# Turning keys, queries and attention outputs by DMA transposes in the second half of a windowed-attention and gMLP kernel

## The chip, the cores and the metric

The kernel runs on one core of a Trainium2 chip. The metric is the device time of one execution in microseconds; a profile of one execution gives a span and the work of each engine: PE (TensorE), DVE (VectorE), ACT (ScalarE), POOL (GpSimd) and SP (SyncE, which here only issues DMAs).

## The reference

Attention over 4 batches of 8 heads, 768 tokens and 64 columns a head, with a window of 128 tokens and 4 tokens at the start ("sinks") that every query sees. The result x, 768 x 512 for each batch, goes through a gated feed-forward block.

```python
scores = scale * np.matmul(q, k.transpose(0, 1, 3, 2))
keep = is_sink | in_window            # rel >= 0 and rel < 128, or token < 4
a = softmax(where(keep, scores, -1e9))
x = np.matmul(a, v)                   # heads side by side: 768 x 512
h = gelu_tanh(x @ w_in)               # 768 x 1024
u, v = h[:, :512], h[:, 512:]
v_n = (v - mean) / sqrt(var + 1e-6) * g_ln
gated = u * (w_sg @ v_n + b_sg[:, None])
out = x + gated @ w_out
```

## The kernel before, in words

Two heads make a pair, so there are 16 pairs n = 0 to 15, four to a batch ("block"). HP is 4, NP is 16, NT is 6 (row tiles of 128 tokens). A pair's work is this:

- load: one DMA each for k, q and v, 384 KB in f32. With the order "(p t)" a partition gets six tokens that follow each other, 1,536 bytes in one run; with "(t p)", used for v alone, a partition gets one token of every row tile, six runs of 256 bytes a head. The pool has three buffers for each of k, q and v.
- cast: to bf16, on POOL (G in the code) for all but the first pairs.
- columns: TensorE turns k, and then q, in six 128x128 transposes into a PSUM bank; ACT (A) or DVE (V) copies the bank into kT or qT, [128 columns of two heads, 768 tokens], putting the tokens back in order. kT and qT have two buffers each.
- score: three groups (0, 1, 2) of matmuls into PSUM, each followed by ACT's exp into ex.
- keep_band: what lies outside the window is set to zero, group 0 by a multiplication with a mask on DVE, groups 1 and 2 by selects on POOL.
- values: two halves (c = 0, 1) of matmuls of ex with v; DVE divides by the sum and writes x (x_sb).
- turn_x: TensorE turns the x of the pair in six transposes, DVE copies the bank into xT.

The feed-forward of a block follows when its four pairs are done: open_v and hidden (x times w_in, gelu on ACT, mean and variance on DVE, the normalised vn), and then units called fillers: spatial (w_sg times vn, then gv and gT on DVE) and project (gT times w_out, an output DMA). Fillers of block b are placed, by fill(), between the attention steps of the pairs of block b + 1. The order on every engine is the order in which the code issues; no scheduler moves anything.

The main loop runs over n = 4 to 15 (L653). In iteration n, PE scores pair n, computes values of pair n - 1, turns k and q of pair n + 1 (L670, L678) and x of pair n - 1 (L688), and POOL casts k, q and v of pair n + 2 (L681). At n = 8 and n = 12 ("block") hidden() of the block just ended runs inside the iteration, with values, columns and turn_x of the running pair called between its units (L693). Loads of pair n + 3 are issued at the head of the iteration (L657). All loads, and all outputs but one, are issued by SP, in this order; an instruction of SP that waits holds back what follows.

PSUM tiles of the tag m (transposes, values, feed-forward) share four banks; scores have two tiles of their own. Outputs go through o_sb, six buffers.

Of the kernel before, what the change touches and what calls it, by code (L numbers as in the profile page):

```python
# [9 lines left out]
BF16 = mybir.dt.bfloat16  # L10
# [8 lines left out]
def kernel(  # L19
# [14 lines left out]
    nc = tc.nc  # L34
    V, G, A = nc.vector, nc.gpsimd, nc.scalar

    B, H, S, Dh = q.shape
# [5 lines left out]
    NT = S // 128  # L43
    HP = H // 2
    KD = DM // 128
    KU = DF // 128
    NP = B * HP
# [8 lines left out]
    work = ctx.enter_context(tc.tile_pool(name="work", bufs=2))  # L56
# [28 lines left out]

        nc.sync.dma_start(out=gates[:, i, :], in_=behind)

    def load(n, which, eng=None):
        b, hp = divmod(n, HP)
        src = dict(k=k, q=q, v=v)[which]  # L90
        dst = loads.tile([128, 2, NT, 64], F32, name=which + "_sb")
        order = "h (t p) d -> p h t d" if which == "v" else "h (p t) d -> p h t d"
        (eng or nc.sync).dma_start(
            out=dst, in_=src[b, 2 * hp:2 * hp + 2].rearrange(order, t=NT))
        raw[n, which] = dst

    flat = {}

    def cast(n, which, eng):
        src = raw.pop((n, which))  # L100
        if which == "v":
            eng.tensor_copy(v_bufs[n % NV][:, :, :, 0:64], src)  # L102
            return
        dst = work.tile([128, NT, 128], BF16, name=which + "_bf")
        eng.tensor_copy(dst.rearrange("p t (h d) -> p h t d", h=2), src)  # L105
        flat[n, which] = dst
# [27 lines left out]
    for i in range(WARM):  # L134
# [3 lines left out]
        out=halves[:, :, 0, :], in_=halves[:, :, 0, :], compare_op=ALU.is_ge, fill=DARK,  # L138
        base=0, pattern=[[0, 2], [1, 128]], channel_multiplier=-1)
    G.affine_select(  # L140
        out=halves[:, :, 1, :], in_=halves[:, :, 1, :], compare_op=ALU.is_ge, fill=DARK,
# [44 lines left out]
    def turn_weights(si, eng):  # L186
        ps = bank([128, NT, 128], BF16, "wps")
        for ti in range(NT):
            nc.tensor.transpose(ps[:, ti, :], wsg_sb[ti // HT][:, ti % HT, 128 * si:128 * (si + 1)],
                                iden)  # L190
        if eng is A:
            A.copy(wsgT[:, si, :], ps.rearrange("p t c -> p (t c)"))
        else:
            eng.tensor_copy(wsgT[:, si, :], ps.rearrange("p t c -> p (t c)"))


    def bank(shape, dtype, name):
        return ps_m.tile(shape, dtype, name=name, tag="m")

    kTs, qTs, exps, avs = {}, {}, {}, {}  # L200
    x_sb, xT = {}, {}

    def columns(n, which, eng):
        src = flat.pop((n, which))
        ps = bank([128, NT, 128], BF16, which + "ps")
        for t in range(NT):
            nc.tensor.transpose(ps[:, t, :], src[:, t, :], iden)  # L207
        dst = work.tile([128, S], BF16, name=which + "T")
        o, i = dst.rearrange("c (p t) -> c p t", t=NT), ps.rearrange("c t p -> c p t")
        if eng is A:  # L210
            A.copy(o, i)  # L211
        else:
            eng.tensor_copy(o, i)  # L213
        (kTs if which == "k" else qTs)[n] = dst

    def darkened(n, g):
        return n < HP or (n == HP and g == 0)

# [39 lines left out]
    def keep_band(n, g, eng):  # L258
        if darkened(n, g):
            return  # L260
        ex = exps[n][:, g, :].rearrange("p (l c) -> p l c", l=2)
        w = 512 if g < HT - 1 else 384
        if eng is V:
            m = mask0 if g == 0 else mask
            V.tensor_mul(ex[:, :, 0:w], ex[:, :, 0:w],
                         m[:, 0:w].unsqueeze(1).to_broadcast([128, 2, w]))
            return
        half = ex[:, :, 0:512].rearrange("p l (j s c) -> p l j s c", j=2, s=2)
        diag, prev = half[:, :, :, 0, :], half[:, :, :, 1, :]
        if g == HT - 1:  # L270
            prev = prev[:, :, 0:1, :]
        nj = prev.shape[2]
        eng.affine_select(out=diag, in_=diag, compare_op=ALU.is_ge, fill=0.0, base=0,  # L273
                          pattern=[[0, 2], [0, 2], [1, 128]], channel_multiplier=-1)
        eng.affine_select(out=prev, in_=prev, compare_op=ALU.is_ge, fill=0.0, base=-1,
                          pattern=[[0, 2], [0, nj], [-1, 128]], channel_multiplier=1)

    def begin_x(b):
        x_sb[b] = work.tile([128, HP, NT, 128], BF16, name="x", bufs=3)
        xT[b] = work.tile([128, HP, S], BF16, name="xT")  # L280

    def values(n, c):
        b, hp = divmod(n, HP)
        if hp == 0 and c == 0:
            begin_x(b)
        ex, v_sb = exps[n], v_bufs[n % NV]
        av = bank([128, HT, 2, 65], F32, "av")

        def probs(j, l, half):
            at = 512 * l + 256 * (j % 2) + 128 * half  # L290
            return ex[:, j // 2, at:at + 128]

        first = True
        for m in range(HT):
            i = HT * c + m
            for l in range(2):
                for j, half in ((i, 0), (i - 1, 1)):
                    if j >= 0:
                        nc.tensor.matmul(av[:, m, l, :], probs(j, l, half), v_sb[:, l, j, :],  # L299
                                         start=first, stop=False)  # L300
                        first = False
        for l in range(2):
            sinks = ex[:, HT - 1, 512 * l + 384:512 * (l + 1)]
            to, of = (av[:, 2, l, :], 0) if c == 0 else (av[:, :, l, :], slice(1, 4))
            nc.tensor.matmul(to, sinks, vsink[:, of, n, l, :], start=False, stop=l == 1)  # L305
        rcp = rcps[:, n, c].rearrange("p (i l o) -> p i l o", l=2, o=1)
        V.reciprocal(rcp, av[:, :, :, 64:65])
        V.tensor_mul(  # L308
            x_sb[b][:, hp, HT * c:HT * (c + 1), :].rearrange("p i (l d) -> p i l d", l=2),
            av[:, :, :, 0:64], rcp.to_broadcast([128, HT, 2, 64]))  # L310

    def turn_x(n, eng):
        b, hp = divmod(n, HP)
        ps = bank([128, NT, 128], BF16, "xps")
        for t in range(NT):
            nc.tensor.transpose(ps[:, t, :], x_sb[b][:, hp, t, :], iden)  # L316
        if eng is A:
            A.copy(xT[b][:, hp, :], ps.rearrange("p t c -> p (t c)"))
        else:
            eng.tensor_copy(xT[b][:, hp, :], ps.rearrange("p t c -> p (t c)"))  # L320


    uTs, vns, gTs, v_alls, mvs, rstds = {}, {}, {}, {}, {}, {}
# [207 lines left out]
    def fill(count=1):  # L531
        for _ in range(count):
            if fillers:
                fillers.pop(0)()
# [114 lines left out]

    QUOTA = {4: 3, 5: 3, 6: 3, 7: 2, 8: 1, 9: 3, 10: 3, 11: 3, 12: 3, 13: 3, 14: 3, 15: 3}  # L650
    LAST = NT + 2 * KU - 1
    valued = HP - 1
    for n in range(HP, NP):  # L653
        todo = valued < n - 1
        block = n % HP == 0 and n > HP
        if HP + 3 < n + 3 < NP:
            for which in "kqv":  # L657
                load(n + 3, which)
        if n not in exps:
            score(n, 0, 1)  # L660
        if n == HP:
            for si in range(3, NT):
                turn_weights(si, V)
        keep_band(n, 0, V)
        keep_band(n, 1, G)
        if todo:
            values(n - 1, 0)
        fill(1 if todo else 2)
        if n + 1 < NP and not block:
            columns(n + 1, "k", A)  # L670
        score(n, 2)
        keep_band(n, 2, G)
        if todo:
            values(n - 1, 1)
        if QUOTA[n] > 2 and todo:
            fill()
        if n + 1 < NP and not block:
            columns(n + 1, "q", A if todo else V)  # L678
        if n + 2 < NP:
            for which in "kqv":  # L680
                cast(n + 2, which, G)  # L681
        if QUOTA[n] > 1:
            fill()
        if block:
            open_v(n // HP - 1, 0)
            open_v(n // HP - 1, 1)
        if todo:
            turn_x(n - 1, V)  # L688
        if block:
            open_v(n // HP - 1, 2)  # L690
        valued = n - 1
        if block:
            hidden(n // HP - 1, {1: [lambda: values(n, 0)], 3: [lambda: values(n, 1)],  # L693
                                 5: [lambda: columns(n + 1, "k", A)],
                                 7: [lambda: columns(n + 1, "q", A)], 9: [lambda: turn_x(n, V)],
                                 LAST: [lambda: score(n + 1, 0, 1), lambda: fill(2)]})
            valued = n
    fill()
# [8 lines left out]
    hidden(B - 1, {2: [lambda: seen.update(c=count_good())],  # L707
                   LAST: [lambda: fill(3)]})
    seen["t"] = total(seen["c"])
# [41 lines left out]
```

## Time and profile before

| | |
|---|---|
| time, median of 3 runs | 174.23 us (173.96 to 179.46) |
| the profiled execution | 173.74 us, span 171.9 us, granted PE clock 0.998 |
| PE / DVE / ACT / POOL busy | 161.0 / 134.3 / 114.1 / 75.1 us |
| DMA queue of SP and ACT (q1) | 25.11 MB, 51.7% of 16 engines' span |
| k and q turns (L207), PE | 96 + 96 matmuls |
| x turns (L316), PE | 96 matmuls |

Busy time counts instructions at work, so an engine that is busy may still be waiting for nothing that matters; what sets the end is in the chain of waits. A row of a stage table gives the stretch in microseconds, then its length, then the busy time of each engine with the number of instructions, the granted clock, the busy share of the DMA engines and the rate that they moved. Lines such as L391 are lines of the kernel.

### The profile page before, as it was taken

The page shows a single profiled execution, that of the slowest core. Times are in us where ns is not written, and L with a number is a line of the kernel's source. Part 1 is how long each engine was busy: PE and PEld are TensorE (multiplying, and loading weights), DVE is VectorE, ACT ScalarE, POOL GpSimd, SP SyncE. Part 2 cuts the span into 40 slices and gives each one's busy share as a digit, 9 for nine tenths or more (in the row PEclk, how much of TensorE's full clock was granted, in tenths as well). Part 3 has the DMA queues.
Part 4 walks back from the last instruction along what each step waited for, and adds up shares of the span by engine and source line. Part 5 has one row for each costly group of instructions (what it writes and reads, how often), then busy time and mean ns, then how long its engine had stood idle before and what let it go on. Part 6 is the DMA issues. An engine that isn't in the chain of part 4 may idle for free.

```text
span 171.9 us, 4205 instructions
## 1 busy us (share of the span) xinstructions
PE 161.0 (94%) x1638; PEld 96.8 (56%) x1638; DVE 134.3 (78%) x321; ACT 114.1 (66%) x155; POOL 75.1 (44%) x112
## 2 busy tenths in 40 slices
PE   3989999999899999999999999999999999999970
PEld 3544584565566666565667655564576645555530
DVE  6675575989999986699889993989989969888630
ACT  2189856889687689597886865789787428631130
POOL 6448461124898969600279987000494400000000
PEclk9999999999999999999999999999999999999999
DMA  4999989999999999700199959000300040040243
GB/s 143 328 323 251 182 112 281 202 275 284 308 235 313 277 276 353 178 0 4 67 320 300 259 148 345 35 0 4 122 4 0 28 159 2 0 183 2 99 170 118
DMA packets 40355, 28.75 MB, mean 167 GB/s; under 512 B 26468, under 2 KB 37240, under 8 KB 40328
## 3 DMA queue, kind: packets, MB, share of 16 engines
q1 hardware_dynamic: 36960, 25.11, 51.7%
q0 software_dynamic: 2944, 2.77, 10.0%
q10 hardware_dynamic: 424, 0.53, 0.9%
q8 instruction: 15, 0.25, 0.6%
q14 instruction: 12, 0.10, 0.2%
HBM read 24.81 MB, written 6.29 MB: 181 GB/s over the span
## 4 chain that ended last, share of the span: by engine, by line
PE 76%; DVE 17%; issue 2%; ACT 1%; POOL 0%; POOLq 0%; DVEq 0%
PE vs L391 15%; PE o_ps L422 12%; PE hu L353 9%; PE hv L334 8%; PE av L299 7%; PE sc L243 6%; PE xps L316 3%; DVE qT L213 3%; PE hv L341 3%; PE kps L207 2%; DVE gT L397 2%; DVE vn L381 2%; DVE st L345 2%; PE qps L207 2%; PE av L305 2%; DVE gv L394 2%
## 5 line engine op out<-in xcount | busy, mean ns | idle before, releaser
L256 ACT ACTIVATE ex<-sc 128x1024 bf16<-128x1024 f32 x48 | 47.6, 1024 | 10.9 <-PE sc L243 7.2
L391 PE MATMUL vs<-wsgT,vn 128*128 128x384 bf16 x192 | 35.5, 326 | 0.3
L273 POOL TENSOR_SCALAR_AFFINE_SELECT ex<-ex 128x512 bf16<-128x512 bf16 x24 | 15.9, 663 | 36.6 <-ACT ex L256 29.8
L391 PEld LDWEIGHTS <-vn 128*128 128x128 bf16 x192 | 17.8, 98 | 11.3 <-issue 0.7
L422 PE MATMUL o_ps<-w_out_sb,gT 128*128 128x512 bf16 x92 | 23.3, 379 | 0.0
L353 PE MATMUL hu<-xT,w_in_sb 128*128 128x384 bf16 x128 | 22.4, 326 | 0.0
L394 DVE SCALAR_TENSOR_TENSOR gv<-vs,g_sb,b_bc 128x384 bf16<-128x384 f32 x32 | 19.6, 612 | 3.2 <-PE vs L391 2.9
L343 ACT ACTIVATE v_all<-hv 128x512 f32<-128x512 f32 x24 | 13.3, 599 | 11.5 <-PE hv L341 11.1
L345 DVE BATCH_NORM_STATS2 st<-v_all 128x6 f32<-128x512 f32 x24 | 16.1, 671 | 4.1 <-ACT v_all L343 4.1
L334 PE MATMUL hv<-w_in_sb,xT 128*128 128x512 bf16 x72 | 18.9, 379 | 0.0
L308 DVE TENSOR_TENSOR x<-av,rcps 128x384 bf16<-128x384 f32 x32 | 17.8, 558 | 1.1
L356 ACT ACTIVATE uT<-hu 128x384 bf16<-128x384 f32 x32 | 15.7, 493 | 3.9 <-PE hu L353 3.4
L397 DVE TENSOR_TENSOR gT<-gv,uT 128x384 bf16<-128x384 bf16 x32 | 16.7, 523 | 1.9
L102 POOL CAST v_sb<-v_sb 128x768 bf16<-128x768 f32 x15 | 13.9, 929 | 9.6 <-PE hu L353 6.2
L243 PE MATMUL sc<-qT,kT 64*128 64x256 bf16 x192 | 15.7, 263 | 1.5 <-DVE qT L213 1.5
L105 POOL CAST k_bf<-k_sb 128x768 bf16<-128x768 f32 x15 | 12.7, 845 | 9.7 <-DMA k_sb<-in_k_dram 9.6
L431 ACT COPY o_sb<-o_ps 128x512 f32<-128x512 f32 x13 | 7.4, 592 | 14.0 <-PE o_ps L428 12.5
L353 PEld LDWEIGHTS <-w_in_sb 128*128 128x128 bf16 x128 | 12.2, 98 | 7.5
L299 PE MATMUL av<-v_sb,ex 128*128 128x65 bf16 x352 | 15.8, 194 | 0.0
L211 ACT COPY kT<-kps 128x768 bf16<-128x768 bf16 x15 | 12.0, 797 | 5.3 <-PE kps L207 5.0
L299 PEld LDWEIGHTS <-ex 128*128 128x128 bf16 x352 | 13.1, 98 | 3.9 <-issue 2.1
L105 POOL CAST q_bf<-q_sb 128x768 bf16<-128x768 f32 x15 | 14.0, 935 | 2.5 <-DMA q_sb<-in_q_dram 2.5
(91 smaller groups left out, 241.8 us busy)
## 6 DMA issues: line engine op xcount, KB each, us to landing
k_sb<-in_k_dram SPq DMA_DIRECT2D x16, 384.0 KB
v_sb<-in_v_dram SPq DMA_DIRECT2D x16, 384.0 KB
out_dram<-o_sb SPq DMA_DIRECT2D x23, 256.0 KB
q_sb<-in_q_dram SPq DMA_DIRECT2D x15, 384.0 KB
wsg_sb<-in_moe_w_sg_dram POOLq DMA_DIRECT2D x2, 576.0 KB, 12.0
w_in_sb<-in_moe_w_in_dram POOLq DMA_DIRECT2D x2, 256.0 KB, 6.6
w_in_sb<-in_moe_w_in_dram POOLq DMA_DIRECT2D x1, 512.0 KB, 6.8
w_out_sb<-in_moe_w_out_dram POOLq DMA_DIRECT2D x1, 512.0 KB, 9.3
```

The lines of the kernel that those rows point to most:

```text
L105: eng.tensor_copy(dst.rearrange("p t (h d) -> p h t d", h=2), src)
L243: nc.tensor.matmul(sc[:, 512 * l + w:512 * l + w + n_q], kT[rows, 128 * j:128 * (j + 1)], qT[rows, 128 * j:128 * j + n_q], start=not dark, ...
L256: A.activation(out=exps[n][:, g, :], in_=sc, func=AF.Exp, scale=scale)
L299: nc.tensor.matmul(av[:, m, l, :], probs(j, l, half), v_sb[:, l, j, :], start=first, stop=False)
L308: V.tensor_mul(x_sb[b][:, hp, HT * c:HT * (c + 1), :].rearrange("p i (l d) -> p i l d", l=2), av[:, :, :, 0:64], rcp.to_broadcast([128, HT ...
L334: nc.tensor.matmul(hvs[b, j], xT[b][:, c, 128 * j:128 * (j + 1)], w_in_sb[:, c, DF:], start=(c == 0), stop=False)
L345: V.bn_stats(out=st, in_=v_alls[b][:, j, :])
L353: nc.tensor.matmul(h_ps[:, 0:NH], w_in_sb[:, c, 128 * f:128 * (f + 1)], xT[b][:, c, NH * n:NH * (n + 1)], start=(c == 0), stop=(c == KD - 1))
L391: nc.tensor.matmul(vs[:, 0:NH], vns[b][:, si, 128 * f:128 * (f + 1)], wsgT[:, si, cols], start=(si == 0), stop=(si == NT - 1))
L394: V.scalar_tensor_tensor(out=gv, in0=vs[:, 0:NH], scalar=g_sb[:, f:f + 1], in1=b_bc[:, cols], op0=ALU.mult, op1=ALU.add)
L397: V.tensor_mul(gTs[b][:, f, cols], gv, uTs[b][:, f, cols])
L422: nc.tensor.matmul(o_ps, gTs[b][:, c, rows], w_out_sb[:, c, :], start=(c == 0), stop=(c == KU - 1 and not by_act))
```

## The change

Keys and queries of pairs 10 to 15 (FIRST = 10) are loaded in the order "(t p)", as v is, and cast as before. In place of columns, one DMA transpose each for k and q, issued by SP, writes kT and qT of pair n + 2 from the cast tiles; no copy out of PSUM follows. For that the casts of k and q of pair n + 2 move ahead, between keep_band of group 1 and that of group 2. The x of pairs 8, 9, 10, 12, 13 and 14 is turned by a DMA transpose into xT, in place of turn_x; pairs 11 and 15 keep the turn on PE, and pairs 0 to 9 keep columns.

Loads: up to pair 11 they are issued at the same places as before; pair 12's moves from the head of iteration 9 to that of iteration 8, pair 13's from the head of iteration 10 into the feed-forward part of iteration 8, pair 14's from the head of iteration 11 to that of iteration 10, and pair 15's from the head of iteration 12 into its feed-forward part. On SP the transposes, loads and outputs of this half stand in the order: loads 11 and 12, an output, kT and qT 10, load 13, xT 8, two outputs, kT and qT 11, load 14, xT 9, kT and qT 12, xT 10, kT and qT 13, two outputs, kT and qT 14, two outputs, load 15, xT 12, two outputs, kT and qT 15, xT 13, xT 14, the other outputs.

```diff
+    FIRST = 2 * HP + 2
...
-    def load(n, which, eng=None):
+    def load(n, which, eng=None, in_rows=False):
...
-        order = "h (t p) d -> p h t d" if which == "v" else "h (p t) d -> p h t d"
+        order = "h (t p) d -> p h t d" if which == "v" or in_rows else "h (p t) d -> p h t d"
...
+    def columns_by_dma(n):
+        for which, Ts in (("k", kTs), ("q", qTs)):
+            src = flat.pop((n, which))
+            dst = Ts[n] = work.tile([128, S], BF16, name=which + "T")
+            nc.sync.dma_start_transpose(out=dst.rearrange("c (t p) -> c t p", t=NT),
+                                        in_=src.rearrange("p t c -> p (t c)"))
...
+    def turn_x_by_dma(n):
+        b, hp = divmod(n, HP)
+        nc.sync.dma_start_transpose(
+            out=xT[b][:, hp, :].rearrange("c (t p) -> c t p", t=NT),
+            in_=x_sb[b][:, hp].rearrange("p t c -> p (t c)"))
...
+    def x_by_dma(n):
+        return n >= 2 * HP and n % HP < HP - 1
+
+    def load_all(m):
+        for which in "kqv":
+            load(m, which, in_rows=m >= FIRST)
+
+    def ahead(n):
+        return [lambda: load_all(n + (5 if n == 2 * HP else 3))] if n >= 2 * HP else []
...
-        if HP + 3 < n + 3 < NP:
-            for which in "kqv":
-                load(n + 3, which)
+        if HP < n <= 2 * HP:
+            load_all(n + 3)
+        if n == 2 * HP:
+            load_all(n + 4)
+        if n == 2 * HP + 2:
+            load_all(n + 4)
...
         keep_band(n, 1, G)
+        turned = FIRST <= n + 2 < NP
+        if turned:
+            cast(n + 2, "k", G)
+            cast(n + 2, "q", G)
...
-        if n + 1 < NP and not block:
+        if n + 1 < min(NP, FIRST) and not block:
             columns(n + 1, "k", A)
...
         if todo:
             values(n - 1, 1)
+            if x_by_dma(n - 1):
+                turn_x_by_dma(n - 1)
+        if turned:
+            columns_by_dma(n + 2)
...
-        if n + 1 < NP and not block:
+        if n + 1 < min(NP, FIRST) and not block:
             columns(n + 1, "q", A if todo else V)
         if n + 2 < NP:
-            for which in "kqv":
+            for which in "v" if turned else "kqv":
                 cast(n + 2, which, G)
...
-        if todo:
+        if todo and not x_by_dma(n - 1):
             turn_x(n - 1, V)
...
-                                 5: [lambda: columns(n + 1, "k", A)],
-                                 7: [lambda: columns(n + 1, "q", A)], 9: [lambda: turn_x(n, V)],
+                                 5: [] if n + 1 >= FIRST else [lambda: columns(n + 1, "k", A)],
+                                 6: ahead(n),
+                                 7: [] if n + 1 >= FIRST else [lambda: columns(n + 1, "q", A)],
+                                 9: [lambda: turn_x_by_dma(n) if x_by_dma(n) else turn_x(n, V)],
```

## The prediction

> **What bounds the kernel now.** I read the page's busy line first, then the chain of waits in order of time, then busy time by stage.
>
> ```profile
> PE 161.0 (94%) x1638; PEld 96.8 (56%) x1638; DVE 134.3 (78%) x321; ACT 114.1 (66%) x155; POOL 75.1 (44%) x112
> PE 76%; DVE 17%; issue 2%; ACT 1%; POOL 0%; POOLq 0%; DVEq 0%
> ```
>
> PE is busy 94% of the span and makes three quarters of the chain; no DMA is in it. From 64 us on the change acts, so I read the chain there (start, length, what). Pair 9's end and pair 10:
>
> ```profile
> 84.53 0.81 DVE gT L397
> 85.34 0.54 DVE gv L394
> 85.90 0.36 DVE gT L397
> 86.26 0.88 DVE qT L213
> 87.18 0.61 PE sc L243 x8
> ...
> 89.25 0.34 PE kps L207 x6
> ...
> 91.65 0.33 PE qps L207 x6
> 91.98 0.98 PE vs L391 x6
> 92.96 0.33 PE xps L316 x6
> ```
>
> Each group of six TensorE transposes is in the chain for 0.33 to 0.34 us, back to back with other PE work. At 86.26 the chain leaves PE: the score of pair 10 waits for the copy of its q columns, behind gv and gT on DVE. Now the stages, one row from the scores of one pair to those of the next (us, then busy us of PE, PEld, DVE, ACT, POOL, clock, DMA share, GB/s):
>
> ```profile
> 80.05:87.18 7.13, 6.96 (x61) 3.88 (x61) 6.45 (x13) 6.41 (x8) 1.38 (x3) 1.00 0.28 90
> 87.18:93.29 6.11, 6.11 (x84) 4.29 (x85) 5.38 (x12) 4.45 (x5) 6.11 (x10) 1.00 1.14 326
> 93.29:99.22 5.93, 5.93 (x83) 4.00 (x84) 5.76 (x12) 4.46 (x5) 5.84 (x9) 1.00 1.02 243
> 104.14:117.00 12.86, 12.85 (x109) 7.49 (x108) 9.39 (x32) 9.82 (x17) 2.05 (x3) 1.00 0.33 100
> ```
>
> PE has no gap in pairs 10 and 11 and in the block's feed-forward part, so time taken from PE there is time taken from the end, until the next engine: DVE, 5.38 to 5.76 us of 6. POOL is as full, but only because its casts lie late; its work is out of the chain.
>
> **What is removed.** Pairs 10 to 15 lose their k and q turns (12 groups of six) and pairs 8, 9, 10, 12, 13, 14 the turn of x (6 groups): 18 groups x 0.335 us = 6.03 us of PE, all on the path. ACT loses six kT copies (797 ns) and four qT copies (799 ns), 8.0 us; it is not the bound, nothing. DVE loses six xT copies of 552 ns and the qT copies of pairs 10 and 14 (0.95 us each): 5.2 us. Of these only the two qT copies are in the chain. PE's last work before 87.18 ends at 86.94, so with the copy gone its gap of 0.24 us goes too: 2 x 0.24 = 0.5 us. Together 6.5 us.
>
> **What of it is not kept.** Without its transposes PE needs 6.11 - 1.0 = 5.11 us for pair 10, DVE still 5.38 (the xT copy of pair 9 lies in the next row). PE can run ahead of DVE, since the four PSUM banks of tag m now serve five uses in an iteration and not eight; I take 0.2 us lost in each of pairs 10, 11 and 14: 0.6 us. In the feed-forward part of block 2, DVE ends vn 0.55 us earlier (the xT copy in the middle of it is gone) while PE arrives 1.0 us earlier; PE had 0.2 us to spare, so 0.3 us is lost. Kept: 6.5 - 0.9 = 5.6 us.
>
> **What is added.** (1) Row loads. k and q of six pairs come in runs of 256 B, as v does already, in place of 1,536 B. Two rows of the same view, one us each; in the first k is moved, in the second v (the last number is GB/s):
>
> ```profile
> 53.00:54.00 1.00, 1.00 (x22) 0.74 (x22) 0.97 (x3) 0.61 (x1) 1.00 (x2) 1.00 1.08 362
> 69.00:70.00 1.00, 0.99 (x8) 0.28 (x6) 0.43 (x1) 0.15 (x2) 1.00 (x3) 1.00 1.17 271
> ```
>
> 393 KB take 1.09 us at 362 GB/s and 1.45 us at 271: 12 loads x 0.36 = 4.4 us more of the DMA queue. It hides: pairs 10, 11 and 12 are now loaded one after the other from 61 us, about 13.1 us of loads and 2 us of outputs, done by 77; the first score of pair 10 is due at 86. Before, the queue was empty from 72 to 85. SP passes pair 11's and 12's loads ahead of an output whose o_sb is one of six buffers: nothing.
>
> (2) 18 DMA transposes of 128x768 bf16, 197 KB. The trace of before has none. Call T the time from one to the next, whether the queue or SP's issue sets it. From below: 197 KB at 362 GB/s, 0.54 us. From above: if every 2-byte element had its own packet at the price of a 256 B one (1.45 us / 1,536 x 16 = 15 ns on each of 16 engines), 98,304 / 16 x 15 ns = 92 us. Read and written pieces are both 256 B runs, so the v row is the nearest: 0.73 us; crossing partitions will not be free, and I take T = 1.0. An output issued at 84.34 shows its first bytes near 85.2, so a transpose lands 0.85 + T after its issue.
>
> The Trainium skill has two figures that disagree. DMA: Bandwidth & Descriptors, "Latency and other measured facts", gives DMA transposes an effective 261 GB/s, which would be an estimated 0.75 us each and changes nothing. VectorE: DVE Perf Modes, "The three transpose paths", lists 1309 ns for one 128x128 block by DMA against 390 ns by TensorE; six blocks in a row would be an estimated 7.9 us. No run shows either yet; the second is what the slower rival below would look like at its worst.
>
> (3) Where they are due, by the new clock. Pair 10's lie behind the loads to 77 us: 9 us to spare. Pair 11's: q is cast by 86.6 (POOL's mask select of pair 9 begins at 83.9, two selects of 0.64, then casts of 0.82 and 0.94), k by 85.7. Landing: 85.7 + 0.85 + 2T = 88.6; its score is due at 91.2 (93.29 less 2.05 saved so far). Pair 12's is the narrow one. The load of pair 14, issued ahead of it on SP, runs from 88.6 for 3 x 1.45 us to 93.0; then xT of pair 9, kT and qT of pair 12: 93.0 + 3T = 96.0, due at 96.4. In general 91.0 + 5T against 96.4. Pairs 13 and 14 have a feed-forward part of 12 us in between. Pair 15 is like 11. xT of pair 14: x is written at 134.83, first needed at 138.4 - 0.33; 0.85 + T = 1.85 of 3.2 us. With 0.4 us for the narrow place: kept 5.2 us.
>
> (4) The k and q casts of the pair two ahead now stand before the mask select of group 2 on POOL. Behind them waits that select, and for it values(n, 1) on PE. At pair 8 the select ends near 70.8 and PE reaches values(8, 1) at 71.42: hidden by 0.6 us; elsewhere 0.6 to 2 us. If that cover goes, 0.5 us for each of four pairs.
>
> **Sum.** The profiled execution took 173.74 us (span 171.9): 173.74 - 5.2 = 168.5. The median of the runs shown is 0.5 above it: 169.0 us.
>
> **Rivals.**
> DVE takes the path. For: 5.76 of 5.93 us in pair 11, and gaps of 0.3 to 0.5 us where DVE waits for ACT's exp. If PE gains nothing from being ahead, pairs 10, 11 and 14 save 0.2 us each in place of 0.8, and pair 9 and 13 half of 0.9: 5.2 - 1.8 - 0.9 = 2.5 saved, 171.7 us. Against: DVE itself loses 5.2 us.
>
> One transpose late. At T = 2 the q of pair 12 lands at 101.0, 4.6 us late; PE stands, in order, at its scores. 5.6 - 4.6 = 1.0 saved, 173.2 us. For: a load of three times 1.45 us goes ahead of it. The other places still hold at T = 2.
>
> The queue is too slow; this is the slower side. One mechanism: kT and qT are made serially behind casts, two iterations of 5 us ahead, and PE waits at the scores. At T = 4, four times my price, pair 11 is 3.3 us late, pair 12 11.3, pair 15 3.3, xT of pair 14 1.7: 19.6 - 5.6 = 14 us more, 188 us. It decides from T = 2.1 (no gain) and costs over 2% from T = 2.6, 181 us at 2.9. For: nothing in the trace turns data by DMA, and 18 of them queue with loads and outputs on one ring of SP. Against: the run length and the 271 GB/s row. The 1309 ns of the skill's table, if it holds for every block, belongs here.
>
> **How the numbers follow.** Forecast (T below 1.5): 0.55. DVE path 0.08, one late transpose (T from 1.5 to 2.6) 0.12; both within 2%, which is about what a measurement of this kernel can tell from no change (3.5 us). Queue too slow 0.25. So faster 0.55, same 0.20, slower 0.25. The likeliest case's own range is 167.3 (all 6.5 us kept) to 171; to hold eight in ten the range must reach into the slow case, to T = 2.9: 167.3 to 181.
>
> **What would show it.** Right: no idle of PE before L243 ended by a DMA, transposes of about 1 us each, stages of pairs 10 and 11 at 5.1 to 5.4 us, no kps or qps after pair 9. Wrong: scores of pairs 11, 12 or 15 that wait for kT or qT from a DMA; PE idle behind gv or mask on DVE; SP's transpose issues of several us. The prediction falls if T is above 2.

## The result, and the profile after

The changed kernel takes 183.21 us (median of 6 runs, 179.37 to 186.02) against 176.69 us for the kernel before, run beside it (median of 6 runs, 173.96 to 180.89). The ratio is 1.035, with a 95% interval of 1.029 to 1.042: 3.5% slower. (All ratios here are taken over the faster runs of each kernel, so they can differ from the ratio of two medians.) The forecast was 169.0 us, and the time is outside its range. Most kernels here, the one before too, vary by up to 7 us from one execution to the next, much of it ahead of pair 8 where nothing was changed; so the profiles are compared from the start of pair 8's scores on, and the last experiments return to the variation.

The profiled execution took 186.02 us with a span of 184.2 us. Its page answers the busy line and the chain of before:

```profile
PE 158.8 (86%) x1512; PEld 91.6 (50%) x1530; DVE 134.2 (73%) x313; ACT 106.7 (58%) x145; POOL 74.1 (40%) x112
PE 21%; DVE 13%; DMA 4%; ACT 1%; POOL 1%; issue 1%; ACTq 0%
```

PE lost only 2.2 us of busy time where 6 us of matmuls were taken out: some of what is left ran slower. DMA, absent from the chain before, is in it. The stages, with the columns of the stage table of before (pairs 9, 10, 11, then 12 with its feed-forward part, then 14):

```profile
86.05:92.34 6.29, 6.24 (x48) 3.11 (x48) 5.47 (x11) 5.57 (x8) 2.31 (x4) 1.00 1.36 167
92.34:98.93 6.59, 5.17 (x65) 3.04 (x64) 6.22 (x13) 3.11 (x4) 6.59 (x10) 1.00 1.16 249
98.93:108.64 9.71, 4.95 (x61) 2.89 (x62) 5.10 (x12) 2.96 (x3) 6.00 (x9) 0.91 1.27 197
108.64:127.59 18.95, 18.77 (x145) 10.19 (x147) 11.81 (x36) 11.62 (x18) 4.51 (x7) 0.87 0.81 172
133.87:138.91 5.04, 5.04 (x65) 3.04 (x64) 4.88 (x10) 3.11 (x4) 5.04 (x8) 1.00 0.73 110
```

Pair 9 takes 6.29 us (7.20 before) and pair 14 takes 5.04 (6.04): the forecast saving is there, a full microsecond an iteration. In pair 11 PE has work for 4.95 us, as forecast, and the stage lasts 9.71. In the next stage the clock is 0.87. What PE waited for (total, times, longest):

```profile
PE sc L253 <- DMA qT<-q_bf: 6.2, 2, 4.7
PE vs L407 <- DVE x L318: 5.1, 1, 5.1
PE hv L350 <- DMA xT<-x: 1.4, 1, 1.4
PE hv L350 <- ACT v_all L359: 0.7, 1, 0.7
```

The first row is what the prediction named as the sign that it is wrong. Its two waits are the scores of pair 11 (1.49 us) and of pair 12 (4.72). The second row lies ahead of pair 8. SP's order around pair 12, from the timeline (start, length, what; "SPq" is SP issuing):

```profile
90.95 2.59 SPq L334 DMA_TRANSPOSE xT<-x  x1
93.64 1.00 SPq L448 DMA_DIRECT2D out_dram<-o_sb  x2
94.74 1.27 SPq L223 DMA_TRANSPOSE kT<-k_bf  x1
96.09 1.23 SPq L223 DMA_TRANSPOSE qT<-q_bf  x1
97.38 0.57 SPq L95 DMA_DIRECT2D k_sb<-in_k_dram  x1
98.00 0.71 SPq L95 DMA_DIRECT2D q_sb<-in_q_dram  x1
98.81 1.64 SPq L95 DMA_DIRECT2D v_sb<-in_v_dram  x1
100.55 2.59 SPq L334 DMA_TRANSPOSE xT<-x  x1
103.24 1.87 SPq L223 DMA_TRANSPOSE kT<-k_bf  x1
105.21 1.24 SPq L223 DMA_TRANSPOSE qT<-q_bf  x1
```

The two transposes of pair 11 take 1.27 and 1.23 us to issue and start 1.35 us apart. Those behind the load of pair 14 take 2.59 and 1.87 us to issue, so qT of pair 12 is not issued before 105.21. PE, in order, stands at the scores until 108.71:

```profile
102.97 1.03 PE L438 MATMUL o_ps<-w_out_sb,gT 128*128 128x512 bf16 x3
108.71 1.04 PE L253 MATMUL sc<-qT,kT 64*128 64x256 bf16 x8 [4.72 <-DMA qT<-q_bf]
```

Eight such matmuls took 0.61 us before (87.18 in the chain that the prediction shows). The granted clock is the reason (last three numbers: clock, DMA share, GB/s):

```profile
104.00:106.00 2.00, 0.00 (x0) 0.00 (x0) 1.29 (x3) 0.00 (x0) 2.00 (x4) 1.00 1.32 121
106.00:108.00 2.00, 0.00 (x0) 0.00 (x0) 0.00 (x0) 0.00 (x0) 0.37 (x1) 0.73 1.16 174
108.00:110.00 2.00, 1.29 (x14) 0.84 (x15) 0.00 (x0) 0.50 (x1) 0.00 (x0) 0.50 0.90 178
110.00:112.00 2.00, 2.00 (x14) 0.77 (x11) 1.36 (x3) 1.44 (x2) 0.44 (x1) 0.50 0.75 175
```

So the wait is paid a second time, as slow matmuls after it. The last feed-forward part has two losses of its own, which stand one behind the other in the chain of waits (start, length, what):

```profile
144.35 4.37 DMA xT<-x
...
148.77 1.04 PE hv L350 x4
...
151.25 1.28 ACT L359
```

The transpose of pair 14's x takes 4.37 us from its issue to landing, with nothing ahead of it in the queue, and PE waits 1.41 us of that. Then comes a load of ACT's table for gelu (L359), 1.28 us. In the timeline of before it ran right behind the last exp, while ACT had nothing else to do:

```profile
133.79 1.28 ACT L343 ACT_TABLE_LOAD   x1
```

Now it stands behind the first hv of the block, and gelu, the mean and variance on DVE and vn wait for it.

Of each profiled execution, the time from the start of one pair's scores to that of the next, in us, worked out from the starts of the first score matmuls (L253; L243 in the kernel before, L255 in e4 and e9). "15" runs to the end of the span, "8 to end" is the sum, and "4 to 8" is the stretch ahead of the change:

| kernel | 8 | 9 | 10 | 11 | 12 | 13 | 14 | 15 | 8 to end | 4 to 8 |
|---|---|---|---|---|---|---|---|---|---|---|
| before | 16.05 | 7.20 | 6.04 | 5.93 | 17.77 | 7.19 | 6.04 | 41.77 | 107.99 | 24.25 |
| after | 15.71 | 6.29 | 6.59 | 9.71 | 18.94 | 6.29 | 5.04 | 45.23 | 113.80 | 30.84 |
| e1_load14_behind | 15.71 | 6.29 | 6.95 | 5.76 | 18.03 | 6.29 | 5.14 | 42.65 | 106.82 | 30.56 |
| e3_order_and_x | 15.71 | 6.29 | 6.89 | 4.93 | 17.67 | 6.29 | 5.44 | 43.27 | 106.49 | 29.49 |
| e4_rows_on_pe | 16.05 | 6.96 | 6.20 | 5.93 | 17.77 | 6.96 | 6.20 | 41.94 | 108.00 | 30.65 |
| e5_clock_kept | 15.71 | 6.29 | 7.00 | 10.09 | 16.77 | 6.29 | 5.04 | 44.59 | 111.77 | 30.24 |
| e6_table_early | 15.71 | 6.29 | 6.59 | 4.93 | 17.77 | 6.29 | 5.07 | 42.21 | 104.85 | 28.69 |
| e7_load13_behind | 15.71 | 6.29 | 5.40 | 6.77 | 18.39 | 6.29 | 5.35 | 42.33 | 106.53 | 26.05 |
| e8_kq_only | 18.06 | 6.29 | 5.39 | 6.72 | 17.11 | 6.29 | 5.50 | 43.64 | 108.98 | 30.57 |
| e9_x_only | 15.71 | 6.96 | 5.90 | 5.81 | 17.44 | 6.96 | 5.90 | 42.02 | 106.70 | 29.73 |
| e10_quiet_start | 15.71 | 6.29 | 7.04 | 4.93 | 17.61 | 6.29 | 5.04 | 42.87 | 105.78 | 25.39 |
| e11_before_quiet | 16.04 | 7.19 | 6.04 | 5.93 | 17.77 | 7.19 | 6.05 | 42.27 | 108.49 | 24.81 |
| e12_load14_columns | 15.71 | 6.29 | 7.21 | 9.10 | 18.26 | 6.29 | 5.06 | 44.46 | 112.37 | 30.74 |
| e13_after_quiet | 15.71 | 6.29 | 7.67 | 9.28 | 19.50 | 6.29 | 5.04 | 44.53 | 114.30 | 24.85 |

Against before, the change gains 3.15 us in stages 8, 9, 13 and 14 (0.34 + 0.91 + 0.90 + 1.00) and loses 8.96 in 10, 11, 12 and 15 (0.55 + 3.78 + 1.17 + 3.46): 5.81 us more. The theory to test (A in the expectations): the loss is one queue's order, transposes that stand behind loads and other transposes on SP, together with the clock that falls while PE waits. The rivals: the row loads, the transposes of x by themselves, the order of the rows in memory.

### The profile page after: what moved, and what is told of

It reads as the page before. It is cut to its first block, busy times and chain, and to the rows that moved or that the text cites. A ratio compares the mean times of both kernels' runs of the same rounds, so it can differ in the third digit from the quotient of the medians.

```text
span 184.2 us, 3978 instructions
## 1 busy us (share of the span) xinstructions
PE 158.8 (86%) x1512; PEld 91.6 (50%) x1530; DVE 134.2 (73%) x313; ACT 106.7 (58%) x145; POOL 74.1 (40%) x112
## 3 DMA queue, kind: packets, MB, share of 16 engines
HBM read 24.81 MB, written 6.29 MB: 169 GB/s over the span
## 5 line engine op out<-in xcount | busy, mean ns | idle before, releaser
L407 PE MATMUL vs<-wsgT,vn 128*128 128x384 bf16 x192 | 37.0, 338 | 5.2 <-DVE x L318 5.1
L413 DVE TENSOR_TENSOR gT<-gv,uT 128x384 bf16<-128x384 bf16 x32 | 21.7, 678 | 2.2 <-DVE gv L410 0.5
L253 PE MATMUL sc<-qT,kT 64*128 64x256 bf16 x192 | 16.3, 272 | 7.0 <-DMA qT<-q_bf 6.2
L369 PE MATMUL hu<-xT,w_in_sb 128*128 128x384 bf16 x128 | 21.9, 326 | 0.0
L107 POOL CAST k_bf<-k_sb 128x768 bf16<-128x768 f32 x15 | 12.9, 861 | 10.9 <-DMA k_sb<-in_k_dram 10.7
L309 PE MATMUL av<-v_sb,ex 128*128 128x65 bf16 x352 | 16.4, 198 | 0.0
L359 ACT ACTIVATE v_all<-hv 128x512 f32<-128x512 f32 x24 | 13.1, 601 | 5.4 <-PE hv L357 4.2
L253 PEld LDWEIGHTS <-kT 64*128 64x128 bf16 x192 | 7.1, 95 | 18.0 <-issue 8.8
L309 PEld LDWEIGHTS <-ex 128*128 128x128 bf16 x352 | 13.6, 100 | 4.2 <-issue 2.3
L107 POOL CAST q_bf<-q_sb 128x768 bf16<-128x768 f32 x15 | 12.7, 845 | 4.2 <-DMA q_sb<-in_q_dram 4.2
```

The costliest lines, as they stand in the source:

```text
L253: nc.tensor.matmul(sc[:, 512 * l + w:512 * l + w + n_q], kT[rows, 128 * j:128 * (j + 1)], qT[rows, 128 * j:128 * j + n_q], start=not dark, ...
L369: nc.tensor.matmul(h_ps[:, 0:NH], w_in_sb[:, c, 128 * f:128 * (f + 1)], xT[b][:, c, NH * n:NH * (n + 1)], start=(c == 0), stop=(c == KD - 1))
L407: nc.tensor.matmul(vs[:, 0:NH], vns[b][:, si, 128 * f:128 * (f + 1)], wsgT[:, si, cols], start=(si == 0), stop=(si == NT - 1))
L413: V.tensor_mul(gTs[b][:, f, cols], gv, uTs[b][:, f, cols])
```

## The experiments

**The order on SP (e1).** Only the place of one load changes:

```diff
-        if n == 2 * HP + 2:
-            load_all(n + 4)
...
             columns_by_dma(n + 2)
+        if n == 2 * HP + 2:
+            load_all(n + 4)
```

> Only the place of pair 14's load on SP changes: behind kT and qT of pair 12 in place of ahead of them. Theory A (the queue's order): in the profile of the changed kernel PE stood 4.7 us at the scores of pair 12 because kT and qT of pair 12 were issued at 103.2 and 105.2 us, behind a load whose bytes took some 5 us of the queue; then this wait falls below 1.5 us, the half clock after it (0.50 to 0.73 in the rows from 106 to 114 us) goes too, and the time falls by 4 to 7 us against the changed kernel, to 173 to 177 us. Theory B (each transpose is slow by itself, 1.23 us of SP and some 4 us from issue to landing, wherever it stands): the wait of pair 12 shrinks by less than 2 us and the time stays at 178 to 181 us.

Measured: 177.09 us (median of 4; the kernel before, run beside it, 177.71), ratio 1.003 with an interval of 0.973 to 1.034. Pair 11's stage falls from 9.71 to 5.76 us, and the long wait is gone; the two waits of the first row are 1.85 us at pair 11 and 0.76 at pair 12, and no half clock follows them:

```profile
PE sc L253 <- DMA qT<-q_bf: 2.6, 2, 1.9
PE hv L350 <- DMA xT<-x: 1.1, 1, 1.1
```

Moving the three DMAs of one load behind three transposes is worth 7.0 us from pair 8 to the end (113.80 to 106.82). The bytes and the number of transfers are the same, so it is the order. The time, 177.09 us, came out at the upper end of what theory A gave. In e3, e6 and e10 below, which keep this order, PE shows no wait for pair 12's transposes.

**The row loads alone (e4).** The loads keep their rows and their new places; all turns are on TensorE again, with a copy that needs no reordering.

```diff
-        return n >= 2 * HP and n % HP < HP - 1
+        return False
...
-        turned = FIRST <= n + 2 < NP
+        turned = False
```

> All turns of k, q and x back on TensorE; the row order of the loads of pairs 10 to 15 and their moved places are kept (the copy out of PSUM is then a plain one). It prices the loads alone. Theory A and B both put the loss in waits for transposes: within 1 us of the kernel before, 173 to 175.5 us. Theory C (the row loads of 256 bytes fill the queue and delay casts or outputs): 2 us or more above the kernel before, with POOL waiting for k_sb or v_sb in front of its selects.

Measured: 177.92 us, ratio 1.007 (0.994 to 1.019); pair 8 to the end 108.00 us against 107.99. Runs of 256 bytes cost nothing that reaches the end when nothing urgent is queued behind them.

**The clock (e5).** The change, with 16 matmuls that nobody reads put ahead of pair 12's scores, in the place where PE waits.

```diff
+        if n == 2 * HP + 4:
+            keep_busy(16)
         if n not in exps:
             score(n, 0, 1)
```

> The changed kernel with 16 matmuls of 512 columns that nobody reads (some 3.5 us) ahead of the scores of pair 12, in the time in which PE stood still. If a stretch of idle PE also costs the granted clock (the rows after the 4.7 us wait show 0.50 to 0.73 for some 6 us), the added work makes the kernel faster than the changed one, by 1.5 to 3 us, and the rows of that stretch show 1.00. If the clock has nothing to do with the wait: no gain, 0 to 1 us slower than the changed kernel.

Measured: 181.99 us, ratio 1.043 (1.029 to 1.057) to the kernel before. Stage 11 is 10.09 us (0.38 more than in the change), but stage 12, at a full clock, is 16.77 us in place of 18.94, and pair 8 to the end is 2.0 us shorter, with 3.5 us of added work. The two stages:

```profile
98.29:108.38 10.09, 8.45 (x80) 4.46 (x82) 4.63 (x11) 2.96 (x3) 5.50 (x8) 1.00 1.30 191
108.38:125.14 16.76, 16.76 (x149) 9.20 (x150) 11.60 (x36) 11.60 (x18) 4.51 (x7) 1.00 0.88 189
```

So about 2 us of the loss are the clock and not the wait itself. As a remedy it is worth little; as a measurement it separates the two.

**Two transposes of x taken back (e3).** e1, with the x of pairs 9 and 14 turned on PE.

```diff
-        return n >= 2 * HP and n % HP < HP - 1
+        return n >= 2 * HP and n % HP < HP - 1 and n not in (9, 14)
```

> As the first of this call, and x of pairs 9 and 14 is turned on TensorE again (12 transposes, 0.67 us of PE back). Theory A: besides pair 12's wait, the 1.4 to 1.9 us wait of the last feed-forward part for xT of pair 14 goes, and xT of pair 9 no longer stands ahead of kT of pair 12: 169.5 to 173 us, faster than the kernel before. Theory B: waits at pairs 11, 12 and 15 remain, 176 to 179 us.

Measured: 175.42 us (median of 4; the kernel before 177.71), which lies between the two expectations: above the 173 us of A and under the 176 of B. The stage of pair 11 is 4.93 us, pair 8 to the end 106.49, 0.3 under e1: two turns of 0.335 us came back on PE and the waits fell by a little more. A wait of 1.43 us remains at pair 11. That xT of pair 14 had to leave the queue is not shown: in e1, with its transpose still there, PE did not wait for it either. The last stage stays at 43.27 us, 1.5 over before, with no transpose of x that PE waits more than 0.72 us for.

**The table load (e6).** e3, and one gelu over 128x1 numbers behind the last exp.

```diff
         score(n, 2)
+        if n == NP - 1:
+            gl = small.tile([128, 1], F32, name="gl", bufs=1)
+            A.activation(out=gl, in_=g_sb[:, 0:1], func=AF.Gelu_apprx_tanh)
```

> As the kernel with the load of pair 14 behind the transposes of pair 12 and x of pairs 9 and 14 turned on TensorE, and in addition one Gelu over 128x1 numbers on ScalarE right behind the last exponential, so that the table of Gelu is loaded there and not behind the first hv of the last feed-forward part. Theory A (the changed kernel lost part of its last part because the 1.28 us table load came to stand on the path from hv to vn): the stage from pair 15's scores to the end falls from 43.43 us to 41.8 to 42.3, so from pair 8's scores to the end 105.0 to 105.6 after 106.65. Rival (the table load lies beside waits that end later anyway): that stage stays within 0.3 us of 43.43.

Measured: 175.47 us (median of 10, 171.93 to 177.02), the kernel before 176.06 (median of 13); ratio 0.991 (0.976 to 1.006). The last stage falls by 1.06 us, to 42.21, as theory A had it; the medians of e3 and e6, 175.42 and 175.47, do not show it. ACT's timeline (start, length, what) shows the load back in ACT's empty time, seven microseconds ahead of the first gelu of the block:

```profile
133.93 1.28 ACT L706 ACT_TABLE_LOAD   x1
135.22 0.20 ACT L706 ACTIVATE gl<-g_sb 128x1 f32<-128x1 f32 x1
141.04 2.71 ACT L359 ACTIVATE v_all<-hv 128x512 f32<-128x512 f32 x5 [5.62 <-issue]
```

**Load 13 moved too (e7).** e6, with the load of pair 13 behind kT and qT of pair 11.

```diff
-                                 6: ahead(n),
+                                 6: ahead(n) if n > 2 * HP else [],
...
+        if n == 2 * HP + 1:
+            load_all(n + 4)
         if n == 2 * HP + 2:
             load_all(n + 4)
```

> As the kernel with the early table, and in addition the load of pair 13 is put behind the transposes of pair 11 instead of into the second block's hidden u part. Theory A (the queue's order: whatever waits on SP ahead of a pair's two transposes delays its scores): PE's wait of 1.4 us for pair 11's qT goes, the stage of pair 10's scores falls from 6.9 to 5.2 to 5.9 us, from pair 8's scores to the end 104.0 to 104.6. Rival (the transposes of pair 11 are late by POOL's casts or by their own landing): the stage of pair 10 stays at 6.6 to 7.0 us. With both, a time of 1.5 to 2.5% under the kernel before.

Measured: 177.00 us (median of 4), ratio 1.014 (0.978 to 1.049). Stage 10 falls to 5.40 us, as theory A had it: the wait of pair 11 was the load ahead of it. But the total is not what was expected. The load now stands ahead of pair 12's transposes, which issue kT only after 3.22 us; 1.8 us of wait and 1.8 us of stage (4.93 to 6.77) come up there, and 1.45 us at xT of the feed-forward part of pair 12. Wherever it goes, a load on this queue is in front of somebody.

**Each half alone (e8, e9).** e8 keeps k and q by DMA and turns all x on PE (x_by_dma returns False). e9 keeps the x by DMA and turns all k and q on PE (turned is False, as in e4).

> The change with x turned on TensorE for all pairs, k and q of the last six pairs by DMA as in the change. Theory A (late transposes of pair 12 behind the load of pair 14, and the clock behind that wait): xT of pair 9 no longer stands between the load and pair 12's transposes, so PE's wait ahead of pair 12's scores falls from 4.7 us by one issue of 1.24 to about 3.4; the waits for xT of pair 14 (1.4 to 1.9 us) and of pair 11's qT (1.4) go or shrink to under 0.5; six groups of 0.335 us come back on TensorE (2.0 us): from pair 8's scores to the end 110 to 111.5 us, still slower than the 108.0 before. Rival B (the x transposes are the loss: they queue against the outputs and hold xT for the last part): 106 to 107.5 us, faster than before.

> Row loads and moved loads kept, k and q of all pairs turned on TensorE, x of the six pairs by DMA as in the change. Theory A: no scores wait for a transpose, six groups of 0.335 us leave TensorE (2.0 us) and 1.4 to 1.9 us come back at the wait for xT of pair 14, nothing lowers the clock: from pair 8's scores to the end 107.3 to 108.2 us beside 108.0 before. Rival B (the x transposes are the loss): 110 us or more.

Measured: e8 180.07 us (ratio 1.023, 0.992 to 1.055), e9 177.74 us (medians of 4 each; before 176.06). The expectation for e8 was wrong in its main term. The load of pair 14 still stands ahead of pair 12's transposes, and yet the wait there is only 0.6 us, not 3.4 (and 4.7 in the change):

```profile
PE hu L369 <- DVE xT L330: 1.9, 1, 1.9
...
PE sc L253 <- DMA qT<-q_bf: 0.6, 1, 0.6
```

Two things make up the difference of 4.1 us, both counted from the start of pair 8's scores. With xT of pair 8 and of pair 9 out of the queue, pair 12's scores can start after 36.5 us and not 38.3, 1.8 us sooner. And PE is ready for them only after 35.9 us and not 33.6, 2.3 us later: stage 8 is longer, where the last hu of the feed-forward part waits 1.85 us for DVE's copy of xT, which the same hu did not do before. (Why that hu waits for the copy here was not followed up.) So part of the wait is not saved but has moved to stage 8. From pair 9 to the end e8 takes 90.92 us, before 91.94, the change 98.09; from pair 8 to the end, with that hu, it takes 108.98, 1.0 us more than before. e9 has no wait for a transpose at all and gains 1.29 us from pair 8 to the end, more than either theory gave it, though its time, 177.74 us, does not show a gain.

So, by the profiles from pair 8 to the end, k and q alone lose 1.0 us, x alone gains 1.3, and both together lose 5.8. Most of what is lost is in their meeting on one queue.

**The order in memory (e12).** The change, with k and q of pair 14 alone loaded in the long runs of before.

```diff
-        order = "h (t p) d -> p h t d" if which == "v" or in_rows else "h (p t) d -> p h t d"
+        order = "h (t p) d -> p h t d" if which == "v" or (in_rows and n != 14) else "h (p t) d -> p h t d"
```

> The change, with k and q of pair 14 alone loaded in the order of before (long runs, 128 descriptors' worth per head and not 256-byte rows); they are then turned into the wrong token order, so what is computed for that pair is not attention, while the work is the same. Theory A (the queue's order and its number of transfers): pair 12's kT and qT still stand behind three loads and xT of pair 9; PE's wait ahead of pair 12's scores falls only by the packets' share, about (1.8 - 1.1) x 2 = 1.4 us, from 4.7 to 3.0 to 3.6. Rival (the row order of the loads by itself fills the queue): the wait falls under 1.5 us and the stage of pair 11's scores to about 6.5 us.

Measured, one run: 184.5 us. The wait ahead of pair 12 is 2.6 us, below what theory A gave and above the rival. But nothing is gained: pair 12's scores start at 108.63 us against 108.71 in the change, and pair 8's had started 0.09 us earlier; PE waits less because it comes later. Pair 11's wait was 2.11 us here (1.49 in the change), and behind it the clock fell:

```profile
98.00:100.00 2.00, 0.47 (x8) 0.36 (x8) 1.38 (x3) 0.00 (x0) 2.00 (x4) 0.97 0.75 129
100.00:102.00 2.00, 2.00 (x20) 1.24 (x17) 0.81 (x3) 1.90 (x2) 0.10 (x1) 0.50 1.06 375
```

Stages 10 and 11 together are 16.31 us, in the change 16.30. Both expectations took the packets for the price; in this one run the runs' length is worth nothing that shows.

**The stretch ahead of the change (e10, e11, e13).** In the profile of the change, one gT multiply on DVE, ahead of pair 8, lasts 7.00 us where its like in the kernel before take 0.36 to 1.2, while POOL runs ten selects and casts without a gap; PE then stands 5.1 us (the second row of its waits above) and comes back at half clock. The kernel with the early table, with pair 4's second mask on DVE and not on POOL:

```diff
-        keep_band(n, 1, G)
+        keep_band(n, 1, V if n == HP else G)
```

> As the kernel with the early table, and in addition the mask of pair 4's second score group is applied on VectorE (one multiply of about 0.7 us) and not by two selects on GpSimd (0.65 us each). This is about the stretch ahead of the change, which is the same in all kernels here: there one gT multiply on VectorE lasted 4.28 or 7.00 us while GpSimd ran ten instructions without a gap, and TensorE then stood idle and came back at a clock of about half. Theory: GpSimd's unbroken run is what holds VectorE; with 1.3 us less of it the gT multiply stays under 1.5 us, from pair 4's scores to pair 8's 24 to 25 us (24.25 in the profile of the kernel before, 28.69 with the early table), from pair 8's to the end 104.5 to 105.2, and the time 169 to 170.5 us with a spread under 3 us, about 3% under the kernel before. Rival: the hold comes from something else, the multiply is held again (4 us or more) and the median stays at 174 to 176 us.

Measured: 172.69 us (median of 10, 171.84 to 173.92), the kernel before 175.75 (median of 13, 173.31 to 180.28); ratio 0.991 (0.986 to 0.997). The same multiply in the change, and then in this kernel (start, length, what):

```profile
46.46 7.00 DVE L413 TENSOR_TENSOR gT<-gv,uT 128x384 bf16<-128x384 bf16 x1
```

```profile
47.85 1.01 DVE L413 TENSOR_TENSOR gT<-gv,uT 128x384 bf16<-128x384 bf16 x1
```

The hold is gone and the spread is 2.1 us. That POOL's unbroken work is what holds the multiply is not shown. The ten profiles with the hold (3.68 to 7.00 us) have POOL at work without a gap from about 43 us on, and the three with the mask on DVE have neither; but the profile of the kernel before has such a run too, eleven instructions from 46.24 to 54.09 us, and its gT multiplies in that run took at most 0.81 us; and in e6 the hold ended at 50.13 us, with POOL's run going on to 53.6. The level of e10 is higher than the expected 169 to 170.5 us: 4 to 8 is 25.39 us, of which the mask's own cost on DVE may be a part, and the last stage came out at 42.87. This is the version that beats both kernels, by 0.9% on the kernel before and, not run side by side, on the changed one (172.69 against 183.21 us). The same line in the kernel before, and in the changed one:

> The kernel before with pair 4's second mask on VectorE, as in the quiet start, and nothing else. Theory (the hold of VectorE under GpSimd's unbroken run made the spread of the kernel before, and is the same with and without the change): the spread falls from 7 us to under 3, from pair 4's scores to pair 8's 24.5 to 26 us, from pair 8's to the end 107.5 to 108.5, median 173.5 to 175. Rival (the spread of before has another cause): the spread stays at 5 to 7 us.

> The changed kernel with pair 4's second mask on VectorE, and nothing else: the change by itself, without the hold ahead of it. Theory A: 4 to 8 in 24.5 to 26 us, from pair 8's scores to the end 112.5 to 114 us as in the changed kernel, median 178.5 to 180.5, so 5 to 6 us or about 3% over the kernel before with the same quiet start. Rival (part of the loss behind pair 8 came from the disturbed start, through the shifted loads): from pair 8 to the end 110 us or less, and a time within 1.5% of the kernel before with the quiet start.

Measured: e11 177.30 us (median of 4, 174.36 to 181.36), e13 179.22 us (176.19 to 181.16), the kernel before 177.30 (7 runs). In both profiles no gT is held and 4 to 8 is 24.81 and 24.85 us. But the spread of e11 is still 7 us: the rival held there. So the hold is not the only source of variation; what the other is stays open, and so does why e10 is free of it. From pair 8 to the end the two profiles differ by 5.81 us (114.30 against 108.49), as with the disturbed start, so in the profiles the start is not what makes the change slow. The times themselves, four runs each, are 1.1% apart by their medians, within the 1.5% that the rival gave, and e13 against the kernel before has a ratio of 1.013 (0.994 to 1.033), lower than the 1.035 of the change. The fastest execution of e13 has a span of 174.5 us. No profile here has pair 8's scores start before 63.9 us; if that holds for this execution too, it took at most 110.6 us from there to the end, 3.7 less than the profiled one. So the loss behind pair 8 seems to vary from one execution to the next, from under 3 us to 6; which of its parts shrinks is open.

## Why the prediction was wrong

**What held.** The saving on PE: 0.9 us in pairs 9 and 13, and 4.9 to 5.1 us for a pair where nothing waits (pair 14 after, pair 11 in e3 and e6), as forecast. DVE did not take the path in the stages; pair 11 of e6 lasts 4.93 us with DVE at 4.20. Only in pairs 14 and 15 of the changed kernel does the chain run on DVE, up to the x that its transpose waits for. The row loads cost nothing (e4). Casts moved ahead of the select of group 2 brought no wait of PE on POOL at pair 8 or later. With the waits and the table mended the sum comes close: forecast 107.99 - 5.2 = 102.8 us from pair 8 to the end, plus 2 x 0.335 for the two x turned on PE again, plus the 1.9 us of waits that e6 still has (1.1 and 0.8), is 105.4; e6 measured 104.85.

**The step that failed** is (3), where the transposes are due: it took a landing of 0.85 + T after the issue, with T = 1.0, and let pair 12's three transposes pass in 3T behind the load. T was a third too small, which alone would not have decided: back to back they are issued 1.32 to 1.35 us apart (1.23 to 1.25 us of SP each). The landing was not: 2.9 us from issue to use for qT of pair 11, 3.5 for pair 12, 4.37 for xT of pair 14 with nothing ahead of it in the queue, where the step had 1.85. And the queue is not a rate alone: behind three row loads SP holds the next transposes at issue for 2.59 and 1.87 us. Pair 12 by the step's own terms, counted from the moment at which PE is ready for pair 11's scores (forecast 91.2; measured 99.00 - 1.49 = 97.51):

| | forecast | measured |
|---|---|---|
| load of pair 14 issued | -2.6 | -0.1 |
| from there to qT of pair 12 landed | 7.4 | 11.3 |
| qT of pair 12 landed | +4.8 | +11.2 |
| PE ready for pair 12's scores | +5.2 | +6.5 |
| PE waits | 0 | 4.7 |

The first line is late by 2.5 us because pair 11's transposes stand behind load 13, xT of pair 8 and two outputs, which the step left out (e7 takes load 13 away, and pair 11's wait goes). The second is 3.9 us longer, 1.0 of it by T (3 x 0.33). PE's own lateness, 1.49 of it pair 11's wait, takes 1.3 back, and the forecast had 0.4 in hand: 2.5 + 3.9 - 1.3 - 0.4 = 4.7.

**Two terms were missing.** The clock: a wait was priced at its own length. e5 puts the slow matmuls behind it at about 2 us. The Trainium skill had the rule: "TensorE: Matmul & The Clock Gate", section "Part 1: The HAM clock gate (the "warmup" mystery)", says that TensorE goes to half rate after about 3.4 us of idling and needs about as long at work to return. The trace agrees with the half (0.50 from 108 to 112 us) but not with the length: 2.11 us of idling in e12 lost the clock. Nor is the length of one wait what decides, since 2.12 us in e7 and 2.57 in e13 kept it at 1.00. In all 14 traces the clock changes only at points that lie a whole number of 3.41 us apart (106.90 and 113.73 in the change lie two of them apart), and the idle time of PE between two neighbouring points is what a change follows. The 2.12 us of e7 (49.90 to 52.02) fall on both sides of such a point, the 2.11 of e12 (97.42 to 99.53) between two. First e7, then e12 (length, PE's busy time; third from the end, the clock):

```profile
47.52:50.94 3.42, 2.38 (x38) 1.49 (x36) 3.42 (x2) 3.04 (x4) 3.18 (x6) 1.00 1.20 222
50.94:54.35 3.41, 2.33 (x19) 1.56 (x20) 3.30 (x8) 0.76 (x1) 3.12 (x5) 1.00 1.15 324
```

```profile
96.48:99.89 3.41, 1.30 (x14) 0.72 (x12) 2.83 (x7) 0.00 (x0) 3.41 (x5) 1.00 0.90 203
99.89:103.30 3.41, 3.41 (x28) 1.53 (x22) 1.67 (x4) 1.94 (x2) 1.35 (x3) 0.50 1.16 324
```

In these traces every stretch of 3.41 us at full clock with over 2.0 us of idling was followed by half clock, none with under 1.6 us was, and in between both occur (e5 lost the clock behind 1.65 us ahead of pair 8 and kept it behind 1.90 us at pair 11); the clock came back behind a stretch with at most 0.33 us of idling. The second term is the table load of 1.28 us, which no line of the diff moves. The three waits (1.49 + 4.72 + 1.41 = 7.6), the clock (2.0) and the table (1.06, from e6) make 10.7 us of the 11.0 by which the profile misses the forecast (113.80 against 102.8).

**The rivals.** The nearest is "one transpose late", whose place was right (pair 12 behind load 14), whose lateness was right within 0.1 us (4.6 forecast, 4.7 measured) and whose time was not: it took T = 2 for the cause and left the other places whole, so it gave 173.2 us. With T at 1.33, that its lateness fits so closely is luck. "The queue is too slow" had the sign and the kind of loss, but its T is not there: at the measured 1.33 us its formula, 91.0 + 5T, gives 97.7 against 96.4 and so a gain. One of its sums is off: by its own terms, with 5.2 us kept, T = 2.9 gives 179.8 us and not 181, which stands for a T of 3.05. As for the figures set against each other in the Trainium skill, the estimate of 0.75 us from "DMA: Bandwidth & Descriptors" ("Latency and other measured facts") is below the measured 1.33 from one issue to the next (197 KB in 1.33 us are 148 GB/s), and 1309 ns for each block, from "VectorE: DVE Perf Modes" ("The three transpose paths"), an estimate of 7.9 us, is not borne out. Neither decided: the price was in latency and order.

## What to carry to other kernels

Work moved to a DMA queue is not off the path: write down the queue's order, and for the narrowest use add the issue of everything ahead of it and the landing of a lone transfer, measured, before calling it hidden. A wait of PE costs more than its length once the clock falls behind it. Two changes that gain or lose little alone can lose much together on one queue, so try each alone and count from ahead of both, and look in the trace of after for instructions that no line of the diff moves, such as a table load.

## What the runs showed of the hardware that was not expected

- A DMA transpose of 128x768 bf16 takes SP 1.21 to 1.27 us to issue when nothing holds it; behind three loads with 256-byte runs, the next one took 2.59 us (the change) and 3.34 us (e8). From the start of its issue to its landing one took 4.37 us with nothing ahead of it in the queue (the change, xT of pair 14).
- TensorE's granted clock went to 0.50 behind 2.11 us of idling (e12) and 4.72 us (the change) and stayed at 1.00 behind 2.12 us (e7) and 2.57 us (e13): it changed only at points a whole number of 3.41 us apart, by the idle time between two of them. At 0.50 eight score matmuls took 1.04 us in place of 0.61.
- One multiply of two bf16 tensors on DVE took 4.28 us (e6) and 7.00 us (the change) while POOL ran without a gap, and 1.01 us in e10, where POOL's run is broken up; a run of eleven POOL instructions in the kernel before did not hold its like, so the cause is open.
